# Three queues for the first loads of a fused adaLN, attention and GLU kernel

## The chip, the core and the metric

The kernel runs on one core of a Trainium2 chip. The metric is the device time of one execution in microseconds (us), taken as the median of several runs. A core has a matrix engine (PE, with weight loads as PEld), a vector engine (DVE), an activation engine (ACT), a general engine (POOL, or GpSimd) and a queue processor for transfers (SP, or SyncE). ACT and POOL can issue transfers too, in their own instruction stream, between their computations. Each engine works through its own list of instructions in order and waits on semaphores of the others.

## The reference

One transformer block on 2048 tokens of width 576. A vector c of 576 elements gives six modulation vectors, two of which shift and scale the normalised input of each half, and one of which gates its output:

```
mod = (silu(c) @ w_mod).reshape(1, 6, 1, 576)      # sa, ca, ga, sb, cb, gb
h = layernorm(x) * (1 + ca) + sa
x = x + ga * A(h)     # 32 heads of 18, each token sees 8 tokens at distance 0, 2, ..., 14
h = layernorm(x) * (1 + cb) + sb
x = x + gb * B(h)     # (h @ w_gate) * (h @ w_up) @ w_down, inner width 4608
```

So nothing of the first half can be projected before c has gone through silu and the first two column blocks of w_mod (the opening's `wmA`, 576 rows by 1152 columns) have been multiplied with it.

## The kernel before

The 2048 tokens are worked in eight chunks of 256 (two tiles of 128 each), and the GLU runs over groups of chunks: 1, 2, 2, 2 and 1 of them. The order of the instructions is fixed when the kernel is built: the opening and the first chunks are written out by hand, and the later attention work is woven between the GLU's matmuls by a small planner with hand-set costs. The change does not touch the planner, and the order on PE after the opening stays what it was.

The opening is the code that the change touches. Its pieces, with the lines of the profile:

- c arrives as five rows (`c_row`) by three transfers, issued from ACT (lines 185 and 187). PE transposes it (line 1029), ACT and DVE make silu of it (lines 1033 to 1040) and DVE spreads it to `sc_bc` (line 1041), the weights of the product with w_mod.
- The first chunk of x arrives as two tiles, j=0 and j=1, issued from SP (line 203). DVE takes its statistics (lines 270, 272), ACT the reciprocal deviation (lines 275, 276), and ACT normalises tile 0 (line 287), DVE tile 1 (line 280).
- `wmA` is loaded in four transfers from SP: two "tails", the last 64 rows of the two column blocks (`load_wm_tail`, line 190), and then two big blocks of 256 rows each (line 206, 576 KB each). After these SP issues wqk (lines 174 and 175), the next chunk of x (line 136), wv, wmC, wo and more.
- `mod_columns` multiplies silu(c) with wmA into `pm` (line 328), first the tails, then, after the ten transposes of the normalised x (line 313), blocks 0 and 1 and blocks 2 and 3. ACT copies the result to `mrow` (line 332), PE transposes that (lines 336, 338), DVE adds the constants (lines 342, 345) and so has `modc`. With it ACT and DVE write the modulated `hT` (lines 304, 302), and PE starts the projections `pq` (line 416).
- `keep_busy` (line 199) issues matmuls on zeros, 512 columns each: seven before the transpose of c, seven after it, and a few later on. Their results are not used.
- POOL prepares constants, among them `shifts`, whose middle is the identity for the transposes (lines 221, 222), and zeroed rows of weights.

Transfers that SP and ACT issue take eight completion semaphores in turn. A transfer that is the ninth in line waits, at its issue, until the one that last had its semaphore has landed. Transfers issued from POOL have semaphores of their own.

Of the kernel before, what the change touches and what calls it, by code (L numbers as in the profile page):

```python
# [18 lines left out]
P = 128  # L19
D = 576  # L20
DP = 640
KT = 5
KF = 4
# [11 lines left out]
ST = CH // P  # L35
NB = 512
# [8 lines left out]
def kernel(  # L45
# [13 lines left out]
    nc = tc.nc  # L59
    S = A_x.shape[1]  # L60
    NCH = S // CH
    x_flat = A_x.rearrange("b s d -> (b s) d")
# [28 lines left out]
    def ps(shape, dt, name):  # L91
        return psp.tile(shape, dt, name=name, tag="bank")

    def js(j):
        return slice(j * P, (j + 1) * P)
# [32 lines left out]
    x_in, x_res = {}, {}  # L128
# [9 lines left out]
    def load_res(i):  # L138
        x_res[i] = xres.tile([P, ST, D], BF, name="x_r")
        nc.sync.dma_start(x_res[i][:], x_rows(i))  # L140
# [41 lines left out]

    wmA = sp.tile([P, KT, 2 * D], BF, name="wmA")
    c_row = sp.tile([KT, P], BF, name="c_row")
    nc.scalar.dma_start(c_row[0:KF, :], c[0, 0:KF * P].rearrange("(m p) -> m p", p=P))
    for c0 in (0, 64):
        nc.scalar.dma_start(c_row[KF:KT, c0:c0 + 64], c[:, KF * P:D])
    def load_wm_tail(wm, blk):
        for b in range(2):
            nc.sync.dma_start(wm[64 * b:64 * (b + 1), KF, b * D:(b + 1) * D], w_mod[KF * P:D, (blk + b) * D:(blk + b + 1) * D])  # L190

    maskneg = sp.tile([P, W, H], BF, name="maskneg")
    busy_w = sp.tile([P, NB], BF, name="busy_w")
# [2 lines left out]
    def keep_busy(n, cols):  # L196
        bank = ps([P, NB], F32, "busy")
        for _ in range(n):
            nc.tensor.matmul(bank[:, 0:cols], lhsT=busy_w[:, 0:P], rhs=busy_w[:, 0:cols], start=True, stop=True)

    x_in[0] = xin.tile([P, ST, D], BF, name="x_t")
    for j in range(ST):
        nc.sync.dma_start(x_in[0][:, j, :], x_flat[js(j), :])
    load_wm_tail(wmA, 0)
    for k in (0, 2):
        nc.sync.dma_start(wmA[:, k:k + 2, :], w_mod[k * P:(k + 2) * P, 0:2 * D].rearrange("(k p) n -> p k n", p=P))
    nc.vector.memset(eps[:], EPS)
# [5 lines left out]
    wmB = wmA  # L213
# [813 lines left out]
    keep_busy(7, NB)  # L1027
    pc = ps([P, KT], BF, "pc")
    nc.tensor.transpose(pc[:], c_row[:], ident[0:KT, 0:KT])
    keep_busy(7, NB)  # L1030
    stat0(0)
    rsq0(slice(0, 1))
    nc.scalar.activation(e_f[:], pc[:], ACTF.Exp, scale=-1.0)
# [63 lines left out]
    for dd4 in range(4):  # L1097
        nk = (DH - dd4 + 3) // 4
        wsrc = bass.AP(A_wo.tensor, A_wo.offset + dd4 * D, [[DH * D, H], [4 * D, nk], [1, D]])
        nc.sync.dma_start(wo[dd4 * H:(dd4 + 1) * H, 0:nk, :], wsrc)  # L1100
    load_res(0)
    load_wm_tail(wmB, 3)
    nc.sync.dma_start(wmB[:, 0:KF, :], w_mod[0:KF * P, 3 * D:5 * D].rearrange("(k p) n -> p k n", p=P))
    load_x(2)
    load_wgr()
# [206 lines left out]
    for gi, grp in enumerate(GROUPS):  # L1312
        hh_t = hhp.tile([P, FT * 2 * CH], BF, name="hh")
        n = CH * len(grp)
# [45 lines left out]
```

## Time and profile before

| | |
|---|---|
| median of 3 runs | 543.81 us (543.6 to 544.0) |
| the profiled execution's own time | 544.44 us |
| its span | 542.7 us |
| PE, PEld, DVE, ACT, POOL busy | 99%, 59%, 58%, 46%, 13% of the span |
| first PE instruction | 1.27 us |
| first projection (line 416) | 11.09 us |
| transfers from 1.8 to 2.4, 4 to 5, 6 to 8 us | 198, 116, 404 GB/s |

The span runs from the first to the last instruction; the execution's own time has some 1.7 us beside it. Busy times of PE are modelled: a busy PE may still wait a little inside a group. In the timelines each row is a start, a length (both in us), an engine, a line and an operation, with the output on the left of the arrow and the inputs on the right, and, in brackets, the idle time before it and what ended that. ACTq and SPq are the transfers that ACT and SP issue; their length is the time of the issue on the issuing engine, not of the transfer. "To landing" is counted from the start of the issue.

### The profile page before, as it was taken

The page shows a single profiled execution, that of the slowest core. Times are in us where ns is not written, and L with a number is a line of the kernel's source. Part 1 is how long each engine was busy: PE and PEld are TensorE (multiplying, and loading weights), DVE is VectorE, ACT ScalarE, POOL GpSimd, SP SyncE. Part 2 cuts the span into 40 slices and gives each one's busy share as a digit, 9 for nine tenths or more (in the row PEclk, how much of TensorE's full clock was granted, in tenths as well). Part 3 has the DMA queues.
Part 4 walks back from the last instruction along what each step waited for, and adds up shares of the span by engine and source line. Part 5 has one row for each costly group of instructions (what it writes and reads, how often), then busy time and mean ns, then how long its engine had stood idle before and what let it go on. Part 6 is the DMA issues. An engine that isn't in the chain of part 4 may idle for free.

```text
span 542.7 us, 14569 instructions
## 1 busy us (share of the span) xinstructions
PE 535.3 (99%) x6157; PEld 321.9 (59%) x6189; DVE 315.9 (58%) x713; ACT 251.5 (46%) x617; POOL 67.9 (13%) x104
## 2 busy tenths in 40 slices
PE   8999999999999999999999999999999999999997
PEld 4887789756745444555544444555544445558875
DVE  4989586777766777646358896524344924032212
ACT  4776777543566553022645552014555551006630
POOL 7104012122000110111000110110010101010210
PEclk9999999999999999999999999999999999999999
DMA  8999999778872694878435983894296592849821
GB/s 264 299 261 363 336 272 332 258 224 258 267 203 89 211 208 153 227 220 293 135 108 163 232 288 68 162 239 159 89 275 176 156 311 69 255 138 294 271 74 42
DMA packets 94924, 114.52 MB, mean 211 GB/s; under 512 B 27980, under 2 KB 83676, under 8 KB 94732
## 3 DMA queue, kind: packets, MB, share of 16 engines
q1 hardware_dynamic: 83360, 67.29, 44.6%
q0 software_dynamic: 11344, 46.25, 27.8%
q8 instruction: 48, 0.79, 0.6%
q14 instruction: 16, 0.13, 0.1%
q10 hardware_dynamic: 156, 0.07, 0.0%
HBM read 103.15 MB, written 4.74 MB: 199 GB/s over the span
## 4 chain that ended last, share of the span: by engine, by line
PE 94%; DMA 3%; DVE 1%; SPq 1%; ACT 1%; issue 0%
PE pg L706 28%; PE pu L706 23%; PE acc L921 19%; PE pq L706 3%; PE accr L926 3%; PE pw L605 3%; PE pq L416 3%; PE acc L976 3%; PE lgT L470 2%; DMA wmC<-in_w_mod_dram 2%; PE pv L706 2%; PE pv L439 1%; DMA wqk<-in_A_wqkv_dram 1%; PE po L567 1%; PE pwj L584 0%
## 5 line engine op out<-in xcount | busy, mean ns | idle before, releaser
L706 PE MATMUL pg<-h2T,wgu 64*128 64x512 bf16 (+1 forms) x1376 | 265.5, 331 | 0.0
L706 PE MATMUL pu<-h2T,wgu 64*128 64x512 bf16 (+1 forms) x1376 | 264.5, 331 | 0.0
L706 PEld LDWEIGHTS <-wgu 64*128 64x128 bf16 x2752 | 136.5, 94 | 94.8 <-issue 0.5
L757 ACT CAST u_sb<-pu 128x512 bf16<-128x512 f32 (+1 forms) x172 | 85.4, 497 | 135.8 <-PE pg L706 131.2
L760 DVE TENSOR_TENSOR hh<-g_sb,u_sb 128x512 bf16<-128x512 bf16 x136 | 57.4, 423 | 116.2 <-ACT g_sb L758 115.7
L758 ACT CAST g_sb<-pg 128x512 bf16<-128x512 f32 (+1 forms) x172 | 86.7, 504 | 0.0
L921 PEld LDWEIGHTS <-hh 128*128 128x128 bf16 x504 | 49.0, 98 | 59.5 <-issue 1.5
L921 PE MATMUL acc<-wd,hh 128*128 128x512 bf16 x329 | 84.1, 380 | 0.1
L926 PE MATMUL accr<-wd,hh 128*128 128x64 bf16 x344 | 62.4, 193 | 0.7
L706 PE MATMUL pu<-h2T,wgr 64*128 64x512 bf16 (+1 forms) x188 | 61.5, 327 | 0.2 <-ACT u_sb L757 0.2
L706 PE MATMUL pg<-h2T,wgr 64*128 64x512 bf16 (+1 forms) x188 | 61.5, 327 | 0.0
L926 PEld LDWEIGHTS <-hh 128*128 128x128 bf16 x504 | 45.8, 98 | 1.9
L171 POOL DMA_DIRECT2D wd<-in_B_w_down_dram x29 | 21.8, 752 | 190.0 <-PE accr L926 93.4
L461 DVE TENSOR_TENSOR prod_t<-qT,kT 128x1280 bf16<-128x1280 bf16 x56 | 43.7, 818 | 0.7 <-ACT kT L777 0.7
L514 DVE TENSOR_TENSOR vsh<-vsh,attn 128x1152 bf16<-128x1152 bf16 x56 | 39.6, 748 | 1.2 <-DMA vsh<-vd 1.2
L706 PEld LDWEIGHTS <-wgr 64*128 64x128 bf16 x376 | 19.7, 94 | 15.4 <-issue 2.5
L921 PE MATMUL acc<-prod_t,hh 128*128 128x512 bf16 x111 | 28.8, 380 | 0.0
L304 ACT ACTIVATE h2T<-h2T,modc 128x256 bf16<-128x256 bf16 x12 | 6.6, 595 | 45.3 <-DMA h2T<-xn 45.3
L455 POOL DMA_DIRECT2D vsh<-vd x14 | 12.5, 897 | 104.8 <-DVE o_sb L524 89.6
L706 PE MATMUL pq<-hT,wqk 64*128 64x256 bf16 (+1 forms) x360 | 22.2, 259 | 0.1
L416 PE MATMUL pq<-hT,wqk 128*128 128x256 bf16 (+1 forms) x225 | 21.2, 251 | 0.4 <-ACT hT L304 0.4
L926 PE MATMUL accr<-prod_t,hh 128*128 128x64 bf16 x112 | 21.6, 193 | 0.1
(208 smaller groups left out, 605.0 us busy)
## 6 DMA issues: line engine op xcount, KB each, us to landing
wgu<-in_B_w_gate_dram SPq DMA_DIRECT2D x41, 512.0 KB, 4.5
wgu<-in_B_w_up_dram SPq DMA_DIRECT2D x41, 512.0 KB, 6.4
wd<-in_B_w_down_dram POOLq DMA_DIRECT2D x29, 576.0 KB, 5.6
vsh<-vd POOLq DMA_DIRECT2D x14, 1152.0 KB, 9.3
prod_t<-in_B_w_down_dram POOLq DMA_DIRECT2D x8, 576.0 KB, 7.6
hh<-in_B_w_down_dram POOLq DMA_DIRECT2D x6, 576.0 KB, 6.4
x_r<-in_A_x_dram SPq DMA_DIRECT2D x8, 288.0 KB, 8.3
vd<-v_sb POOLq DMA_DIRECT2D x16, 144.0 KB, 5.2
```

The costliest lines, as they stand in the source:

```text
L171: return nc.gpsimd.dma_start(wb[:], B_w_down[r0:r0 + FB * P, :].rearrange("(k p) n -> p k n", p=P))
L416: nc.tensor.matmul(pq[:, gi, :], lhsT=wqk[:, kt, m * P:(m + 1) * P], rhs=hT[:, kt, cols], start=(kt == order[0] and not (by_k and gi)), st ...
L461: nc.vector.tensor_tensor(prod, aa[i]["qT"][:], aa[i]["kT"][:, :, off:off + CH], ALU.mult)
L514: nc.vector.tensor_tensor(v, v, at, ALU.mult)
L605: nc.tensor.matmul(pw[:], lhsT=oT[:, m, js(j)], rhs=wo[:, m, 0:512], start=(m == 0), stop=(m == KT - 1))
L706: return nc.tensor.matmul(out, lhsT=lhs, rhs=rhs, start=first, stop=last, skip_group_check=True)
L757: nc.scalar.copy(u[:, c, :], pu)
L758: nc.scalar.copy(g[:, c, :], pg)
L760: return lambda: nc.vector.tensor_tensor(hh[:, f - c:f + 1, :], g, u, ALU.mult)
L921: nc.tensor.matmul(acc[j][:], lhsT=hh[:, f, js(j)], rhs=wb[:, f % FB, 0:512], start=(f == 0), stop=(f == FT - 1))
L926: nc.tensor.matmul(accr[:, j, :], lhsT=hh[:, f, js(j)], rhs=wb[:, f % FB, 512:D], start=(f == 0 and j == 0), stop=(f == FT - 1), skip_grou ...
L976: nc.tensor.matmul(acc[i][:], lhsT=hh[:, f, js(j)], rhs=wb(f)[:, c0:c1], start=(f == 0), stop=(f == FT - 1))
```

## The change

The requests that the opening makes first are spread over three issuing engines and put in another order. SP issues tile 0 of x and then at once the two big blocks of wmA. ACT issues tile 1 of x and the two tails, in place of the three transfers of c. POOL issues c, in two transfers in place of three: the row of c's last 64 elements, which is wanted twice, comes by one transfer that reads it twice. The second batch of fillers shrinks from seven to five. `load_wm_tail` takes the queue as an argument; its later use, for the second pair of blocks, stays on SP.

```
-    nc.scalar.dma_start(c_row[0:KF, :], c[0, 0:KF * P].rearrange("(m p) -> m p", p=P))
-    for c0 in (0, 64):
-        nc.scalar.dma_start(c_row[KF:KT, c0:c0 + 64], c[:, KF * P:D])
-    def load_wm_tail(wm, blk):
+    nc.gpsimd.dma_start(c_row[0:KF, :], c[0, 0:KF * P].rearrange("(m p) -> m p", p=P))
+    nc.gpsimd.dma_start(c_row[KF:KT, :].rearrange("p (t n) -> p t n", t=2), bass.AP(c.tensor, c.offset + KF * P, [[D, 1], [0, 2], [1, 64]]))
+
+    def load_wm_tail(wm, blk, queue):
         for b in range(2):
-            nc.sync.dma_start(wm[64 * b:64 * (b + 1), KF, b * D:(b + 1) * D], w_mod[KF * P:D, (blk + b) * D:(blk + b + 1) * D])
+            queue.dma_start(wm[64 * b:64 * (b + 1), KF, b * D:(b + 1) * D], w_mod[KF * P:D, (blk + b) * D:(blk + b + 1) * D])
...
-    for j in range(ST):
-        nc.sync.dma_start(x_in[0][:, j, :], x_flat[js(j), :])
-    load_wm_tail(wmA, 0)
+    nc.sync.dma_start(x_in[0][:, 0, :], x_flat[js(0), :])
+    nc.scalar.dma_start(x_in[0][:, 1, :], x_flat[js(1), :])
+    load_wm_tail(wmA, 0, nc.scalar)
     for k in (0, 2):
         nc.sync.dma_start(wmA[:, k:k + 2, :], w_mod[k * P:(k + 2) * P, 0:2 * D].rearrange("(k p) n -> p k n", p=P))
...
     nc.tensor.transpose(pc[:], c_row[:], ident[0:KT, 0:KT])
-    keep_busy(7, NB)
+    keep_busy(5, NB)
...
-    load_wm_tail(wmB, 3)
+    load_wm_tail(wmB, 3, nc.sync)
```

## The prediction

> **What bounds the kernel now.** I read the page first (which engine), then what PE waited for, then the chain that ended last, then the timeline of the first 11 us, and last that opening's traffic in stretches.
>
> The page: the span, and PE's share.
>
> ```profile
> span 542.7 us, 14569 instructions
> PE 535.3 (99%) x6157; PEld 321.9 (59%) x6189; DVE 315.9 (58%) x713; ACT 251.5 (46%) x617; POOL 67.9 (13%) x104
> ```
>
> PE's waits over the whole span (line, releaser, total, times, longest):
>
> ```profile
> PE busy L199 <- DVE busy_w L194: 1.3, 1, 1.3
> PE pq L416 <- ACT hT L304: 0.4, 1, 0.4
> ```
>
> PE starts at 1.27 us and then hardly stops. An opening that puts the first projection (11.09 us) forward puts the end forward by as much, if later loads keep up. The chain of waits names two loads in the opening:
>
> ```profile
> 4.11 6.48 DMA wqk<-in_A_wqkv_dram
> ...
> 11.76 8.89 DMA wmC<-in_w_mod_dram
> ```
>
> wqk lands at 10.59, half a us before line 416 starts, and wmC at 20.65, when PE's row for it (line 356) starts at 20.79: wmC has no spare time.
>
> The timeline of the opening:
>
> ```profile
> 0.81 0.55 ACTq L185 DMA_DIRECT2D c_row<-in_c_dram  x1
> 0.82 0.87 SPq L203 DMA_DIRECT2D x_t<-in_A_x_dram  x2
> 1.40 0.53 ACTq L187 DMA_DIRECT2D c_row<-in_c_dram  x2
> 1.74 1.19 SPq L190 DMA_DIRECT2D wmA<-in_w_mod_dram  x2
> 1.96 1.28 ACT L212 ACT_TABLE_LOAD   x1 [1.96 <-issue]
> 2.25 0.68 POOL L226 DMA_DIRECT2D vd<-zrow  x1 [0.30 <-POOL zrow L225]
> 2.97 1.10 SPq L206 DMA_DIRECT2D wmA<-in_w_mod_dram  x2
> 4.09 0.29 ACT L275 ACTIVATE ln_rstda<-ln_mva,eps 128x1 f32<-128x1 f32 x1 [0.85 <-DVE ln_mva L272]
> 4.37 0.18 PE L1029 MATMUL pc<-shifts,c_row 5*128 5x5 bf16 x1
> 4.48 2.68 PE L199 MATMUL busy<-busy_w 128*128 128x512 bf16 x7
> 5.45 0.85 ACT L287 ACTIVATE xn<-x_t,ln_nb,ln_rstda 128x576 bf16<-128x576 bf16 x1
> 5.57 0.26 DVE L1041 COPY sc_bc<-sc 128x160 bf16<-128x160 bf16 x1
> 7.09 0.32 PE L328 MATMUL pm<-wmA,sc_bc 64*32 64x320 bf16 x4
> 8.01 0.46 PE L328 MATMUL pm<-wmA,sc_bc 128*32 128x320 bf16 x8
> ```
>
> The product pm could start once sc_bc is there (5.57 + 0.26 = 5.83) and the tails have landed (1.74 + 2.5 and 2.30 + 2.3, both by 4.6); it starts at 7.09 because the second batch of fillers holds PE. The big blocks land 4.4 after their issue, at 7.37 and 8.00, before PE takes them (8.01 and 8.71). So fillers, not loads, set this path, by 0.6 to 0.7 us. The traffic, with its share and GB/s as the last two columns:
>
> ```profile
> 3.00:4.00 1.00, 1.00 (x4) 0.25 (x2) 0.97 (x4) 0.24 (x1) 1.00 (x2) 1.00 0.60 152
> 4.00:5.00 1.00, 1.00 (x5) 0.34 (x4) 0.97 (x6) 0.64 (x3) 1.00 (x4) 1.00 0.77 116
> ...
> 6.00:8.00 2.00, 2.00 (x18) 0.91 (x16) 0.20 (x2) 0.30 (x1) 1.82 (x5) 1.00 1.04 404
> ```
>
> Until 5 us the transfers run at a third of the 404 that follows: issue is what lacks there.
>
> **The change part by part.** *Two fillers fewer.* The weight loads of the second batch start at 4.88, 5.31, 5.74, 6.16, 6.57: 0.427 apart, the slow pace. The seventh filler starts at 6.78 and takes 0.38 (0.63 for the earlier ones), so the last two already ran at the fast pace; a pair at 9.27 takes 0.61 where one takes 0.39, so fast ones are 0.22 apart. PE comes free 0.10 after a filler ends (6.99 to 7.09). The fifth starts at 6.16 and ends at 6.59, so pm starts at 6.69: 0.40 earlier. Bounds: 0.22 if other work becomes last at once, 0.85 if both dropped ones were slow in the run at hand. I take 0.40, the profiled rows. Covers: sc_bc at 5.83 (spare 0.86); tile 0's normalisation ends at 6.30, tile 1's at 6.15, for transposes at 6.94 (spare 0.64); the big blocks are then wanted at 7.61 and 8.31. Even unmoved (7.37, 8.00) they would be in time.
>
> *Big blocks second on SP.* SP skips one tile of x and two tails: 2.97 - 1.28 = 1.69 us earlier for every SP issue. Landing at 5.7 and 6.3, wqk at 8.9. None of it lies on the path up to line 416, as all had spare time: nothing there. It counts at wmC: PE comes to it at 20.25 in place of 20.65, and the unmoved landing would swallow the gain. wmC's issue hangs on wqk's landing by the ring of eight semaphores (SP waits 1.2 us for wqk ahead of the wv tail, 10.61), and wqk comes up to 1.69 earlier. The ring now makes wqk's main second part wait for the first wmA block (5.7, about when SP gets there) in place of a tail; behind it stand the k columns, wv and wmC, with the k columns wanted from about 14 us. I bound wmC's advance by 0 and 1.69 and take 1.2; anything over 0.40 is enough.
>
> *Tile 1 and tails on ACT.* ACT issued three transfers in 1.08 us; now x (0.40 as on SP, 0.55 as ACT's first) and two tails (0.59 each on SP): 1.7. The table load moves from 1.96 to about 2.6 and ends at 3.9, in front of 4.09, where ACT waits for DVE. Zero cost, by a cover of 0.2; with issues at the 0.85 of SP's slowest here it ends at 4.4, the normalisation is 0.3 later, still inside the 0.64. Tile 1, issued before 0.82 instead of 1.28, is wanted at 3.97; it lands by 3.1. The tails (issue 1.4 and 2.0, landing 2.5 later) are in by 4.5, or by 6.4 with the 4.4 of a big block, still before 6.69.
>
> *c on POOL.* Two issues of 0.68 (the row of vd) stand in front of the constants: the identity is done at 2.8 in place of 1.43, wanted at 4.37; the zeroed kT at 5.9, wanted at 6.11 by a DVE that then idles to 10.37; the rest of sc_bc goes from 11.51 to 12.9, wanted at 20.79. The second c transfer is issued at 1.5; POOL's row of vd took 2.2 to land, so c is in at 3.7, against 4.3 when the first seven fillers end: hidden, spare 0.6. Bounds: 2.2, and 6.0, which a store of v took from POOL amid full traffic (3.7 or 7.5).
>
> [...]
>
> *Sum.* -0.40, with nothing else on the path. The profiled execution is 544.44 (span 542.7); it becomes 544.04 (span 542.3). It stands 0.63 above the median, so the median goes from 543.81 to 543.4. About 0.2% (1.09 us) is what can be told from no change: this gain is below that.
>
> **The rivals.**
>
> *Loads give more (faster).* DVE waits 0.72 for x at 30.23 and 0.70 for v_e at 35.55, in a stretch where it is 90% busy. With loads 1.2 earlier these and the 0.54 of PE's idle time from 16.3 to 100 us could go: -0.40 - 1.42 = 542.0 with the two waits. Against it: PE is shown busy 5.00 of 5.00 us around both. 12%.
>
> *Absorbed.* SP and ACT hinder each other's issue, wmC is no earlier, and PE waits at 20.79 as before: 543.8. The 0.55 for ACT's first tiny transfer beside SP's speaks for it a little. 14%.
>
> *c comes late (slower).* Fillers are in order behind the transpose of c, so each us of landing after 4.37 is a us lost. Beside the big blocks, which now move from about 2.5, the second c transfer may take the store's 6.0: 7.5 - 4.37 - 0.40 = +2.7, 546.5. Slower by over 1.09 from a landing at 5.9 on, 4.4 after issue. Against it: 2.2 for the row of vd, issued into traffic of 262 GB/s. 8%.
>
> *The clock falls back (slower).* Fillers run slow for 5.3 us (1.27 to 6.57). With two fewer, the gaps in PE's work to 10.7 might leave or make the array slow again; one more such stretch at half pace loses 2.65, less 0.40: 546.1. It takes 3.0 us of slow pace to pass 1.09. Against it: the switch comes before the dropped fillers run, and three fillers stay behind them. 6%. [...]
>
> **How the numbers follow.** Forecast 60%, own range 543.0 (0.85 saved) to 543.6 (0.22). Faster by over 0.2%: 12%; slower: 8 + 6 = 14%; within: 60 + 14 = 74%. The range, 542.4 to 544.9, takes in the forecast, the absorbed case and the nearer part of the other three.
>
> **What would show it.** Right: five fillers after c, then pm near 6.7, line 416 near 10.7, wmC landed near 19.4, wmA issued at 1.28, no wait of PE on c_row. Wrong: a gap on PE before line 1029; a table load ending after 4.7; fillers or projections still at the slow pace after 6.6; PE waiting at 20 us; a gain lost again between 11 and 45 us.

## The result, and the profile after

The changed kernel takes 547.93 us (median of 6 runs, 547.87 to 548.32) against 543.83 (6 runs, 543.6 to 544.09): a ratio of 1.0073, interval 1.0063 to 1.0083. It is 4.1 us slower. The forecast was 543.4, 0.4 faster, with a range of 542.4 to 544.9: the time lies outside the range, and on the other side.

The page of the changed kernel: PE is busy as long as before (535.6 against 535.3 us), in a span 3.5 us longer. Nothing became more work; PE stood still, and for part of the opening it ran slowly.

```profile
span 546.2 us, 14566 instructions
PE 535.6 (98%) x6155; PEld 321.8 (59%) x6187; DVE 317.5 (58%) x713; ACT 251.3 (46%) x617; POOL 69.3 (13%) x106
```

What PE waited for, over the whole span: one new row, at the top, with 3.3 us in one piece.

```profile
PE pc L1029 <- DMA c_row<-in_c_dram: 3.3, 1, 3.3
PE busy L199 <- DVE busy_w L194: 1.3, 1, 1.3
PE pq L416 <- ACT hT L304: 0.4, 1, 0.4
```

The chain that ended last, in the opening: where wqk and wmC stood before, there is now the second transfer of c, 0.2 KB that took 5.57 us, and behind it five fillers that took 2.25.

```profile
2.01 5.57 DMA c_row<-in_c_dram
...
7.87 2.25 PE busy L199 x5
...
14.78 0.47 ACT hT L304
```

The timeline of the opening, in the order of the lines shown before:

```profile
0.82 0.41 ACTq L203 DMA_DIRECT2D x_t<-in_A_x_dram  x1
1.27 1.17 ACTq L190 DMA_DIRECT2D wmA<-in_w_mod_dram  x2
1.28 0.93 SPq L206 DMA_DIRECT2D wmA<-in_w_mod_dram  x2
1.35 0.67 POOL L185 DMA_DIRECT2D c_row<-in_c_dram  x1 [0.82 <-POOLq L1344]
2.01 0.56 POOL L186 DMA_DIRECT2D c_row<-in_c_dram  x1
2.47 1.28 ACT L212 ACT_TABLE_LOAD   x1 [2.47 <-issue]
3.90 0.82 DVE L270 BATCH_NORM_STATS2 ln_statsa<-x_t 128x6 f32<-128x288 bf16 x2 [2.51 <-DMA x_t<-in_A_x_dram]
7.71 0.16 PE L1029 MATMUL pc<-shifts,c_row 5*128 5x5 bf16 x1 [3.27 <-DMA c_row<-in_c_dram]
7.80 2.31 PE L199 MATMUL busy<-busy_w 128*128 128x512 bf16 x5
10.05 0.45 PE L328 MATMUL pm<-wmA,sc_bc 64*32 64x320 bf16 x4
11.61 0.72 PE L328 MATMUL pm<-wmA,sc_bc 128*32 128x320 bf16 x8
12.27 0.61 PE L199 MATMUL busy<-busy_w 128*128 128x512 bf16 x1
15.28 5.18 PE L416 MATMUL pq<-hT,wqk 128*128 128x128 bf16 x90 [0.43 <-ACT hT L304]
```

Against before: the transpose of c goes from 4.37 to 7.71, 3.34 later. From there to pm it is 0.38 less (2.34 against 2.72). From pm to the first projection it is 1.23 more: 10.05 to 15.28 against 7.09 to 11.09. The sum is 4.19. The 1.23 is pace: a group of eight pm matmuls takes 0.72 in place of 0.46, a lone filler 0.61 in place of 0.39. The matmuls run as slowly as those of the first microseconds did (the weight loads of the fillers from 7.80 on lie 0.42 to 0.43 apart, as those from 1.68 on do), though the granted clock is shown as 1.00 from 8 to 16 us. The traffic, with share and GB/s last:

```profile
3.00:4.00 1.00, 1.00 (x4) 0.26 (x2) 0.10 (x1) 0.75 (x1) 0.71 (x2) 1.00 1.00 353
4.00:5.00 1.00, 0.44 (x2) 0.00 (x0) 0.97 (x4) 0.00 (x0) 0.95 (x2) 1.00 1.05 402
```

In these two microseconds 353 and 402 GB/s move, where 152 and 116 moved before. The change does what it was meant to do with the bytes: it fills the transfer engines from 3 us on. But c, issued at 1.35 and 2.01, lands in the midst of that traffic, at about 6.1 and 7.58. The second big block, issued at 1.74, takes 6.1 and lands at about 7.85 (KB and us to landing last):

```profile
wmA<-in_w_mod_dram SPq DMA_DIRECT2D x1, 576.0 KB, 6.1
```

Up to 63 us the rows of PE in the two traces lie 4.0 apart. From 83 us to the end they lie 3.3 apart, as the profiled execution of before loses about 0.7 us in between that the other does not. That execution stood 0.6 above its median, so the medians (4.10) give the change's price better than the spans (3.5). Why it lost that stays open. So a difference of half a us in the opening can't be read from the time of one execution.

### The profile page after: what moved, and what is told of

Its sections match the earlier page's. It is cut to its first block, busy times and chain, and to the rows that moved or that the text cites. A ratio compares the mean times of both kernels' runs of the same rounds, so it can differ in the third digit from the quotient of the medians.

```text
span 546.2 us, 14566 instructions
## 1 busy us (share of the span) xinstructions
PE 535.6 (98%) x6155; PEld 321.8 (59%) x6187; DVE 317.5 (58%) x713; ACT 251.3 (46%) x617; POOL 69.3 (13%) x106
## 4 chain that ended last, share of the span: by engine, by line
PE 96%; DMA 1%; DVE 1%; issue 1%; ACT 0%; POOL 0%; POOLq 0%
PE pg L706 28%; PE pu L706 23%; PE acc L921 19%; PE pq L416 4%; PE pq L706 3%; PE accr L926 3%; PE pw L605 3%; PE acc L976 3%; PE lgT L470 2%; PE pv L706 2%; PE pv L439 2%; DMA c_row<-in_c_dram 1%; PE po L567 1%; PE busy L199 1%; PE tr_pA L313 0%
```

## The experiments

The theory after the result: c is late because the big blocks are ahead of it, and the idle PE then runs slow. Rivals: POOL's transfers are slow by themselves; the dropped fillers cost the clock; the tails or tile 1 on ACT are what is late.

**c on SP, ahead of the big blocks.** The changed kernel, with only this:

```
-    nc.gpsimd.dma_start(c_row[0:KF, :], c[0, 0:KF * P].rearrange("(m p) -> m p", p=P))
-    nc.gpsimd.dma_start(c_row[KF:KT, :].rearrange("p (t n) -> p t n", t=2), bass.AP(c.tensor, c.offset + KF * P, [[D, 1], [0, 2], [1, 64]]))
...
     nc.sync.dma_start(x_in[0][:, 0, :], x_flat[js(0), :])
+    nc.sync.dma_start(c_row[0:KF, :], c[0, 0:KF * P].rearrange("(m p) -> m p", p=P))
+    nc.sync.dma_start(c_row[KF:KT, :].rearrange("p (t n) -> p t n", t=2), bass.AP(c.tensor, c.offset + KF * P, [[D, 1], [0, 2], [1, 64]]))
```

> The changed kernel with only c's two transfers moved from POOL to SP, behind tile 0 of x and ahead of the big blocks. Theory A (POOL's late c is the whole loss: PE waited 3.27 us for it, and the idle array then ran slow to about 14 us): c lands by 4.4, PE does not wait at line 1029, the transpose of c starts near 4.4 and the first projection by 11.1, time 543.4 to 543.9. Rival B (the tails on ACT are late too: issued at 1.27 and about 1.85 they landed at about 6.0 and 8.0 in the changed kernel): pm cannot pass the second tail before 8.0, the first projection comes near 12, time 544.5 to 545.0. Rival C (the five fillers in place of seven leave the array slow): fillers still 0.43 apart after c and pm's groups of eight at 0.72 instead of 0.46, time 545 or more.

Measured: 543.75 against 543.89, ratio 0.9993 (0.9983 to 1.0003). The whole loss is gone, with tails and tile 1 on ACT, five fillers and c's form of two transfers still in place. Its timeline:

```profile
4.38 0.18 PE L1029 MATMUL pc<-shifts,c_row 5*128 5x5 bf16 x1
6.49 0.32 PE L328 MATMUL pm<-wmA,sc_bc 64*32 64x320 bf16 x4
9.26 0.46 PE L328 MATMUL pm<-wmA,sc_bc 128*32 128x320 bf16 x8 [0.88 <-DMA wmA<-in_w_mod_dram]
```

c is in time, and pm starts 0.6 earlier than before (6.49 against 7.09), but then PE waits 0.88 for the second big block, and the first projection comes at 11.46, against 11.09 before and the 11.1 expected. The gain is taken by a block that lands at about 9.2. Rival B named the right kind of wait and the wrong transfer.

**c on POOL alone**, in the kernel before:

```
-    nc.scalar.dma_start(c_row[0:KF, :], c[0, 0:KF * P].rearrange("(m p) -> m p", p=P))
-    for c0 in (0, 64):
-        nc.scalar.dma_start(c_row[KF:KT, c0:c0 + 64], c[:, KF * P:D])
+    nc.gpsimd.dma_start(c_row[0:KF, :], c[0, 0:KF * P].rearrange("(m p) -> m p", p=P))
+    nc.gpsimd.dma_start(c_row[KF:KT, :].rearrange("p (t n) -> p t n", t=2), bass.AP(c.tensor, c.offset + KF * P, [[D, 1], [0, 2], [1, 64]]))
```

> The kernel before with only c's transfers moved from ACT to POOL, all else as before (seven fillers, big blocks last on SP). Theory A1 (c is late because it shares the transfer engines with the big blocks that now start at about 2.5 us): here only x and tails run when c is issued at 1.35 and 2.0, so it lands in 2.2 to 2.5, by 4.5; time 543.7 to 544.2. Theory A2 (POOL's small transfers take about 5 us from issue whatever runs beside them): c lands at 7 to 7.6 again, PE waits about 3 us, time 547.0 to 548.8, with seven slow fillers behind it up to 0.85 above the changed kernel.

Measured: 544.51 against 543.89, ratio 1.0008 (0.9997 to 1.0019): no difference that can be told, and a little above the 544.2 expected. The issue row of c's second transfer (KB, us to landing), and then the same row of the changed kernel:

```profile
c_row<-in_c_dram POOLq DMA_DIRECT2D x1, 0.2 KB, 2.2
```

```profile
c_row<-in_c_dram POOLq DMA_DIRECT2D x1, 0.2 KB, 5.6
```

The same transfer on the same engine, issued at the same 2.01 us, takes 2.2 us when the big blocks are issued from 2.97 on, and 5.6 when they go ahead of it. POOL by itself was not slow.

**Doses of the big blocks.** The changed kernel, c on POOL. First with the tails back on SP, ahead of both blocks; then with one block ahead of the tails and one behind:

```
-    load_wm_tail(wmA, 0, nc.scalar)
+    load_wm_tail(wmA, 0, nc.sync)
```

> The changed kernel with the two tails back on SP ahead of the big blocks; c stays on POOL, tile 1 on ACT, five fillers. The big blocks are issued at about 2.45 and 2.95 in place of 1.28 and 1.74. If c is late because of the bytes that the blocks put ahead of it, it lands 1.5 to 3 us sooner than 7.58, by 4.4 to 6, time 543.8 to 545.5. If sharing with another queue, or tile 1 on ACT, delays it, c stays near 7.5 and the time near 547.9.

> The changed kernel with one big block ahead of the tails on SP and the other behind them (issued at about 1.28 and 2.9); c stays on POOL. Half the dose: one block of 576 KB moves in about 1.5 us at the 400 GB/s of the busy stretches, so c lands about 1.5 us sooner than 7.58, near 6, and the time is 545.5 to 546.5. If c waits for both blocks or none, the time stays at 547.9 or falls to 544.

Measured: 544.34 against 544.20, ratio 1.0003 (0.9993 to 1.0013), and 545.71 against 544.20, ratio 1.0028 (1.0017 to 1.0039). PE's wait for c, in the first and in the second:

```profile
PE pc L1029 <- DMA c_row<-in_c_dram: 0.7, 1, 0.7
```

```profile
PE pc L1029 <- DMA c_row<-in_c_dram: 1.7, 1, 1.7
```

c's second transfer, issued at 2.01 each time, takes 3.0 with only tails ahead, 4.0 with one block, 5.6 with two. The more of wmA stood ahead of it, the later c landed, as both expectations had it. Whether the bytes count, or the number of transfers or packets, these two kernels don't tell apart.

**c on ACT, behind tile 1.** The changed kernel with c's two transfers on ACT, issued at 1.27 and 1.88:

```
     nc.scalar.dma_start(x_in[0][:, 1, :], x_flat[js(1), :])
+    nc.scalar.dma_start(c_row[0:KF, :], c[0, 0:KF * P].rearrange("(m p) -> m p", p=P))
+    nc.scalar.dma_start(c_row[KF:KT, :].rearrange("p (t n) -> p t n", t=2), bass.AP(c.tensor, c.offset + KF * P, [[D, 1], [0, 2], [1, 64]]))
     load_wm_tail(wmA, 0, nc.scalar)
```

> The changed kernel with c's two transfers on ACT, behind tile 1 of x and ahead of the tails; the big blocks stay second on SP. If c's place on POOL is the whole loss, c (issued by 1.9) lands by 4.8, PE waits under 0.5 us for it, and with the second block in at about 7.9 (1.74 + 6.1, as in the changed kernel; it came at 9.2 where c stood ahead of it on SP) the first projection starts by 10.6: 543.0 to 543.6, below the kernel before. Rival: what stands on any queue while the big blocks run is late, c here too (4.5 or more after its issue, landing 6 to 6.5), with an idle array and slow matmuls: 545.5 to 547.

Measured: 547.82 against 544.20, ratio 1.0068 (1.0054 to 1.0082). It is as slow as on POOL: the rival's case, and 0.8 above the 547 that the rival allowed. The same with the product taking the tails after the first block:

```
-    add_modc = mod_columns(wmA, 0, lambda: keep_busy(2, NB), {KF: x0_ts, 1: lambda: keep_busy(1, NB)})
+    add_modc = mod_columns(wmA, 0, lambda: keep_busy(2, NB), {0: x0_ts, 1: lambda: keep_busy(1, NB)}, (0, 1, KF, 2, 3))
```

> As the kernel with c on ACT behind tile 1, and the product of silu(c) takes the tails after the first big block instead of first. The tails on ACT landed at 6.0 and 8.0 in the changed kernel, the first block at 5.7, the second at 7.9. If the tails hold the product there, this starts the first projection 0.3 to 1 us earlier than with the tails first, 542.5 to 543.3; if c or the second block holds it, the two are equal.

Measured: 547.57, ratio 1.0058 (1.0043 to 1.0072); c holds PE here too, so the order of the product could show little. PE's wait in this kernel (its lines are numbered one lower; the profiled execution, 546.29, was the quickest of the five):

```profile
PE pc L1028 <- DMA c_row<-in_c_dram: 2.4, 1, 2.4
```

So the engine that issued c hardly mattered here: beside and behind the big blocks the kernel took 547.93 with c on POOL and 547.82 with c on ACT, ahead of them 544.51 and 543.75 with c on POOL and on SP.

**A bridge of fillers**, to part the wait from the pace. The changed kernel with

```
-    keep_busy(7, NB)
+    keep_busy(17, NB)
     pc = ps([P, KT], BF, "pc")
```

> The changed kernel with seventeen fillers ahead of the transpose of c in place of seven, so that PE works through the wait for c. c comes as late as in the changed kernel (7.58). If part of the loss is the clock (the array goes through 3.3 us of idleness and runs slow from 7.8 to about 14: pm to first projection 5.23 instead of 4.00 us, five fillers at 0.43), this gives 545.6 to 546.4: the transpose still at 7.7, then fast fillers, pm near 9.3, first projection near 13.3. If only the wait for c counts, the time stays at 547.9.

Measured: 546.49 against 543.89, ratio 1.0041 (1.0028 to 1.0055), 2.6 above the kernel before where the changed kernel is 4.1. Its timeline:

```profile
1.27 6.33 PE L199 MATMUL busy<-busy_w 128*128 128x512 bf16 x17 [1.27 <-DVE busy_w L194]
7.92 1.25 PE L199 MATMUL busy<-busy_w 128*128 128x512 bf16 x5
9.05 0.83 POOL L244 MEMSET edge<- 16x896 bf16 x1
9.08 0.89 DVE L1041 COPY sc_bc<-sc 128x160 bf16<-128x160 bf16 x1
10.03 0.32 PE L328 MATMUL pm<-wmA,sc_bc 64*32 64x320 bf16 x4 [0.85 <-DVE sc_bc L1041]
```

c comes as late as in the changed kernel, but the five fillers now take 1.25 in place of 2.31 and the first projection starts at 13.85 in place of 15.28. About 1.5 of the 4.1 us come from the slow pace behind an idle PE. The other 2.6 come with the late c; in this kernel they hold 0.85 us in which PE waits for sc_bc. The expectation of 545.6 to 546.4 was missed by a little: sc_bc took 0.89 in place of 0.26 (below).

**Five fillers alone**, in the kernel before:

```
     nc.tensor.transpose(pc[:], c_row[:], ident[0:KT, 0:KT])
-    keep_busy(7, NB)
+    keep_busy(5, NB)
```

> The kernel before with five fillers in place of seven behind the transpose of c, nothing else. The step of the prediction as it stands: pm starts 0.40 earlier (6.69), the first projection at about 10.7, and at PE's row for wmC (20.79) the unmoved landing at 20.65 takes the gain away again: time 543.7 to 543.9, the same. Rival (wmC's landing does not hold PE, or moves with the rest): 543.4. Rival C (the clock needs the two fillers): slower by over 1 us, 545 or more.

Measured: 544.61 against 543.89, ratio 1.0007 (0.9997 to 1.0016): no gain. Its timeline:

```profile
4.48 1.25 PE L199 MATMUL busy<-busy_w 128*128 128x512 bf16 x5
6.46 0.32 PE L328 MATMUL pm<-wmA,sc_bc 64*32 64x320 bf16 x4 [0.73 <-DVE sc_bc L1041]
9.22 0.46 PE L328 MATMUL pm<-wmA,sc_bc 128*32 128x320 bf16 x8 [0.72 <-DMA wmA<-in_w_mod_dram]
```

pm starts 0.63 earlier than before, and PE then waits 0.28 for the first block and 0.72 for the second, which comes at about 9.2. The first projection starts at 11.42, later than the 11.09 of before's profile. The second block takes the step away, long before wmC could. The 0.63 is not the two fillers alone: the five that are left ran at the fast pace here, 1.25 in all, and PE then stood 0.73 for sc_bc, as one small DVE operation ahead of it (line 1037) took 0.62 in place of 0.19.

**Tails on ACT alone**, in the kernel before, which makes the big blocks second on SP with c ahead of all; and the same with five fillers and the tails late in the product:

```
-    load_wm_tail(wmA, 0)
+    load_wm_tail(wmA, 0, nc.scalar)
```

> The kernel before with one part of the change alone: the tails on ACT, behind c's three transfers, which puts the big blocks second to x on SP (issued at about 1.74 and 2.2). c stands ahead of them all and lands near 4.1, as before. The second block comes sooner (8.8 where c was on POOL alone; 7.9 in the changed kernel, issued at 1.74), but the tails, issued behind it on ACT from about 1.95, land 4.7 to 6.2 later, at 6.7 to 8.2. If the early blocks are worth something once c is in time, the time is 543.2 to 543.6; if the tails take the place of the second block as the last to come, it is the same, 543.8 to 544.2.

> As the kernel with the tails alone on ACT, with five fillers behind c, and with the product taking the tails after the first block. If neither fillers nor tails but only the second block is last, pm ends 0.5 to 1 us sooner than before and the time is 542.8 to 543.4. If c or x is late again behind the blocks, it is above 544.

Measured: 545.51 against 544.30, ratio 1.0032 (1.0019 to 1.0045), and 544.16, ratio 0.9997 (0.9987 to 1.0007). In the first, c is in time (the transpose at 4.37) and now the tails are late. (The profiled execution, 546.79, is 1.3 above the median, so these waits may be longer than the usual ones.)

```profile
7.08 0.31 PE L328 MATMUL pm<-wmA,sc_bc 64*32 64x320 bf16 x2 [0.44 <-DMA wmA<-in_w_mod_dram]
9.02 0.45 PE L328 MATMUL pm<-wmA,sc_bc 64*32 64x320 bf16 x2 [1.63 <-DMA wmA<-in_w_mod_dram]
```

The second tail, 72 KB issued behind the blocks, took 6.4 us and landed at about 9.0, near the 8.88 at which PE took the second block before. Both expected times for this kernel were too low. They took the tails for a mere replacement of the second block, but the product takes the tails first, so everything else stands behind them. In the second kernel PE waits 1.28 for the first block, and the second tail is late too (PE waits 0.51 for it, until 10.03), which takes what the order might give. None of these versions is faster than the kernel before.

## Why the prediction was wrong

- *c on POOL* is the step that failed: "c is in at 3.7, against 4.3 ...: hidden, spare 0.6". It landed at 7.58. POOL's issue started at 1.35, not 0.82, and the landing took 5.6, not 2.2. The 2.2 was taken from the row of vd, measured while 116 to 262 GB/s moved; but the change itself raises that traffic to 353 and 402 in the very microseconds in which c travels. The upper bound (6.0, a store of v under full traffic) was the right row: 1.5 + 6.0 = 7.5. That this sum meets 7.58 so closely is luck, as the issue came 0.5 later and the landing took 0.4 less. It was given 8% as "c comes late", with 546.5. The rival's mechanism and place were right, and its chance far too small; its price lacked the pace, about 1.5 us more.
- *The clock* was a rival for the wrong reason. Five fillers were enough (where c was in time or 0.7 late, on SP, in the kernel before, or with only the tails ahead, pm's groups of eight took 0.46). An idle PE is what cost here: behind waits of 1.6 to 3.3 us the matmuls ran slowly, behind waits of up to 1.28 they did not, each in one execution. With the tails alone on ACT a fast pace was lost: a pair of pm matmuls takes 0.31 at 7.08, and 0.45 at 9.02 behind the wait of 1.63. In the changed kernel PE fell idle at 4.44, and with fillers throughout (the bridge) the slow spacing lasted to 6.4; so whether it lost a fast pace or had not reached one is not shown. In the bridge, fillers from 1.27 to 7.60, with a wait of 0.23 behind them, left the next five at 1.25 us in place of 2.31. How long PE has to be busy for the fast pace, or idle to lose it, no run shows.
- *Two fillers fewer, -0.40* was not there. It rested on "the big blocks land 4.4 after their issue, at 7.37 and 8.00". Only the first block's landing is in the trace of before; 8.00 was the first one's duration put on the second. Where the second's is given it took 5.2 (c on POOL alone, landing at 8.8), and 6.1 in the changed kernel. So before, too, it is likely to have come shortly ahead of the 8.88 at which PE used it (an estimate: 3.6 + 5.2 = 8.8), and fillers and second block were about equally late. Five fillers alone gave 1.0007.
- *Big blocks second on SP, nothing on the path* was right in sign for the first block (5.7 as forecast), wrong for the second (7.85, not 6.3), and wrong in kind: it was counted only as earlier landing of the blocks, not as later landing of all else. x came 0.9 later (3.90 against 2.99), the tails at 6.0 and 8.0 and not at 4.5.
- *Tile 1 and tails on ACT*: the table load ended at 3.75, in front of its user, as said. "The tails ... by 6.4 with the 4.4 of a big block" was too kind by 1.6; that cost nothing here, as PE came to the tails only at 10.05, but with the tails alone on ACT, c in time, the kernel was 1.2 us slower than before.
- *wmC* was no limit after the change. PE's row for it starts 0.26 behind the row ahead of it (24.51 and 24.77), as in the kernel with c on SP (20.69 and 20.95). Before, the two lie 0.47 apart (20.32 and 20.79): some 0.2 was waited for wmC there, as the prediction's "no spare time" had it. The ring of eight that its argument on wmC used shows in the traces. Before, SP's and ACT's transfers name eight semaphores and POOL's eight others, and the ninth of SP and ACT, the second big block, names that of the first. In the changed kernel SP waits twice for wmA, 1.9 us in all, and issues parts of wqk at 6.03 and 8.03, as the tails land at 6.0 and 8.0.

## What to carry to other kernels

When a change fills an idle transfer engine, price every small transfer in flight at that time by rows from full traffic, not by rows from the quiet kernel before (here 5.6 us against 2.2); the smallest one, on which the most waits, should be issued ahead of the bulk on whatever queue. Check that a landing you lean on is the one of that very transfer. And PE's early wait cost more than its length here: about 1.5 of the 4.1 us were slow work behind it.

## What was not expected of the hardware

A queue of its own did not protect c. Its second transfer, 0.2 KB on POOL's queue, went from 2.2 to 5.6 us, with two blocks of 576 KB ahead on SP's, and on ACT's queue PE waited 2.4 for c. The trace shows the first packets of POOL's queue (q0) only from 4.9 us on, 2.9 after the end of the first issue; with c on POOL alone, where the issue is the same, 16 of them move between 2.5 and 3.0. So most of the time passes before they move; what holds them back, no run shows.

Two vector operations took longer beside a POOL memset. sc_bc takes 0.26 us before, and 0.89 in the bridged kernel, where it starts 0.03 behind a POOL memset and ends, at 9.97, just after it (9.88). No run takes POOL's memset away, so it is not shown to be the cause. POOL's constants had moved 1.5 us later, and c's late arrival had moved the copy; the prediction costed POOL's move only by who waits for the constants. A longer operation also came without the move: with five fillers alone, line 1037 runs from 5.00 to 5.62 beside a memset from 5.03 to 5.60. Not every one is longer: before, lines 1037, 1038 and 1040 take 0.19, 0.19 and 0.17 between 4.92 and 5.54, beside memsets that run from 4.51 to 5.62.

The slow pace is not in the granted clock, which reads 1.00 in every stretch shown. It also varied: the second batch of fillers was fast from 4.48 on with five fillers alone (five in 1.25), and slow to 6.57 in the kernel before (weight loads 0.43 apart), with the same first seven.
